# Pairs of score tiles that share a threshold and a reciprocal, in an attention and feed-forward kernel

## The chip, the core and the metric

The kernel runs on one core of a Trainium2 chip, as one program in one launch. The core has five engines that work through instruction lists of their own and meet at semaphores: TensorE (PE, matmuls), VectorE (DVE), ScalarE (ACT), GpSimd (POOL) and SyncE (SP, which issues DMAs). The metric is the device time of one execution in microseconds; the median of three runs of the kernel before is 1106.18 us (1106.06 to 1106.43).

## The reference

```python
def _attn_ref(q, k, v, tau):                      # q, k, v: 8 x 8 x 576 x 64, tau = 0.02
    scores = scale * np.matmul(q, k.transpose(0, 1, 3, 2))
    thresh = np.max(scores, axis=-1, keepdims=True) - tau
    scores = np.where(scores >= thresh, scores, -1000000000.0)
    scores = scores - np.max(scores, axis=-1, keepdims=True)
    attn = np.exp(scores)
    attn = attn / (np.sum(attn, axis=-1, keepdims=True) + 1e-09)
    return np.matmul(attn, v)
def _moe_ref(x, w_in, w_out):                     # x: 4608 x 512, w_in: 512 x 2048, w_out: 2048 x 512
    h = x @ w_in
    g = np.where(h >= 1, h, np.where(h <= -1, 0.0, (h + 1) ** 2 / 4))
    return g @ w_out
```

The attention output of each token, all heads beside each other, is the x of the second function. Only the scores within 0.02 of their row's maximum keep a weight.

## The kernel before

The eight batches go one after the other through attention, and the feed-forward part (FFN) follows them token group by token group, so that both are in flight together. Every fp32 factor is split into two fp16 parts, hi and lo, and a product is three fp16 matmuls (hi hi, hi lo, lo hi). Batch 0 alone computes its scores in fp32 (L987), since its split q and k aren't ready.

A score tile is 128 query rows by 576 keys; there are 36 a batch, 288 in all. Two tiles of the fp16 kind are computed together into the two PSUM score buffers (L998, 12 matmuls). `add_tile` then does for each tile by itself: the maximum with its scale on VectorE (`smax`, L1038), the threshold as one 128x1 addition on VectorE (`sthr`, L1042), the exponential on ScalarE (L1045), a mask with the row sum on VectorE, a reciprocal of 128x1 on VectorE, then normalisation and split. The table TILE picks the way of that tail:
- P (the default): the mask reads the scores in PSUM (`smask`, L1064), the reciprocal is L1074, GpSimd normalises (L1082) and takes the rest (L1090), ScalarE makes the hi part (L1087).
- R (batch 0 only): `smax` also writes a copy of the scores to SBUF, so PSUM is free early; the mask reads that copy (`mask_r`, L1050), and the denominator gets its epsilon in an operation of its own (L1078) ahead of its reciprocal (L1079).
- S: mask, hi and rest straight from PSUM, the mask (L1098) and the rest (`lo_s`, L1109) on VectorE, none of it on GpSimd.
- T: one tile that TensorE transposes (`turn_e`, L1129).

Every tile but T's is sent by a transposing DMA (SP, L1112). When a part's tiles are there, `add_av` multiplies with v (L1194; 30 matmuls of 320 columns for the wide parts), and the result is split into the x of the FFN (L1202, L1206). An FFN step is FFN1 (L1266, 12 matmuls per 128 hidden units), two ScalarE operations (L1272, L1275), the gate on VectorE (L1279), and the split of the gate's 512 columns: `ghi` on ScalarE (L1284) and `glo` on VectorE (L1289), each in two operations, one for each half of 256 columns, since the halves lie in buffers of different rings (ga, gb). FFN2 (L1311, matmuls of 512 columns) sums into one PSUM buffer, and the group's tokens are scaled and stored.

The weights arrive as float64 and are converted in 32 tiles of 512 KB; the table CONV picks the engine for each step of each tile, and two of these steps matter here: a rest on VectorE with two inputs from SBUF (`rest2`, L865) and one from PSUM (L884). FSCALE picks the engine of the FFN's eight scale chains.

The order of the work is written out by hand: ORDER lists the numbers of all operations. The class Plan walks it with a cost for each operation, gives out the buffers of each ring, computes a start for each, and issues the program in the order of these starts. An engine executes its own instructions strictly in that order.

Of the kernel before, what the change touches and what calls it, by code (L numbers as in the profile page):

```python
# [1372 lines left out]
```

## Time and profile before

| | |
|---|---|
| median of 3 runs | 1106.18 us |
| profiled execution | 1105.19 us, its span 1103.4 us |
| PE busy | 1066.5 us (97%) |
| DVE busy | 912.6 us (83%) |
| ACT busy | 865.5 us (78%) |
| POOL busy | 724.7 us (66%) |
| mean granted clock of PE | 0.983 of full |

The span runs from the first instruction to the last; the execution's time has 1.8 us more. A share of busy time is an average over the whole span, and the stages differ: a window of the trace shows an engine's busy time in one stretch, a wait shows what released an engine that stood idle. The rows below are of this one execution.

### The profile page before, as it was taken

What the parts mean: (1) busy time and instruction counts of PE and PEld (TensorE: products, weight loads), DVE (VectorE), ACT (ScalarE), POOL (GpSimd) and SP (SyncE); (2) the same over time, 40 slices, a digit from 0 to 9 for tenths busy, and PEclk for the clock granted to TensorE, in tenths of its full rate; (3) what the DMA queues carried; (4) which work ended last, traced back from release to release, by engine and by line L of the source; (5) the groups of instructions that cost most, each with busy time, mean ns of one, the idle gap of its engine ahead of it and who ended that gap; (6) DMA issues with size and microseconds to landing.
All of it is one profiled execution on the core that took longest, in us unless ns stands there. A gap on an engine that the chain in (4) does not pass through costs nothing.

```text
span 1103.4 us, 27341 instructions
## 1 busy us (share of the span) xinstructions
PE 1066.5 (97%) x9827; PEld 721.4 (65%) x9827; DVE 912.6 (83%) x2704; ACT 865.5 (78%) x1651; POOL 724.7 (66%) x829
## 2 busy tenths in 40 slices
PE   6778899999999999999999999999999999999998
PEld 4567557666776666765676676666676676666774
DVE  6999999899989898897998898798778788888231
ACT  6888879798878888888788887788678787687442
POOL 6899998678867787786676654785537577364000
PEclk9679999999999999999999999999999999999999
DMA  9996787858966876688665966597635757575000
GB/s 330 303 290 115 145 175 153 136 119 195 187 111 141 164 164 133 107 178 165 124 120 124 182 126 124 101 179 158 123 75 100 146 102 138 96 119 110 9 20 29
DMA packets 419321, 154.96 MB, mean 140 GB/s; under 512 B 398192, under 2 KB 398192, under 8 KB 419184
## 3 DMA queue, kind: packets, MB, share of 16 engines
q1 hardware_dynamic: 419184, 153.21, 67.7%
q8 instruction: 77, 1.26, 0.5%
q14 instruction: 60, 0.49, 0.1%
HBM read 45.09 MB, written 9.44 MB: 49 GB/s over the span
## 4 chain that ended last, share of the span: by engine, by line
PE 78%; DVE 8%; POOL 5%; issue 3%; DMA 3%; ACT 3%; SPq 0%; DVEq 0%; POOLq 0%; ACTq 0%
PE ph L1266 30%; PE acc L1311 28%; PE ph L1194 9%; PE s L998 9%; POOL e L1082 2%; POOL hl L1090 2%; DMA eT<-hl 2%; DVE e L1064 1%; DVE s L1038 1%; PE s L987 1%; POOL WO L862 1%; ACT hl L1087 1%; ACT e L1045 1%; DMA raw<-in_v_dram 0%; DMA vst<-vb 0%
## 5 line engine op out<-in xcount | busy, mean ns | idle before, releaser
L1266 PE MATMUL ph<-x,WI 128*128 128x256 f16 (+1 forms) x4032 | 401.5, 259 | 2.4 <-DVE x L1206 2.1
L1090 POOL TENSOR_TENSOR hl<-e,hl 128x576 f16<-128x576 f32 x272 | 351.5, 1302 | 71.7 <-ACT hl L1087 68.3
L1266 PEld LDWEIGHTS <-WI 128*128 128x128 f16 x4032 | 346.9, 99 | 61.8 <-issue 19.1
L1082 POOL TENSOR_SCALAR e<-e,sm 128x576 f32<-128x576 f32 x272 | 217.2, 806 | 166.9 <-DVE sm L1074 135.2
L1087 ACT ACTIVATE hl<-e 128x576 f16<-128x576 f32 x272 | 183.5, 681 | 65.6 <-POOL e L1082 54.9
L1038 DVE TENSOR_SCALAR_CACHE_REDUCE s<-s,pc 128x576 f32<-128x576 f32 x252 | 199.1, 821 | 36.9 <-PE s L998 35.7
L1045 ACT ACTIVATE e<-s,sm 128x576 f32<-128x576 f32 x273 | 196.6, 740 | 28.4 <-DVE s L1038 25.5
L1064 DVE SCALAR_TENSOR_TENSOR e<-s,sm,e 128x578 f32<-128x578 f32 x257 | 204.9, 815 | 14.7 <-ACT e L1045 10.8
L1311 PE MATMUL acc<-WO,ga 128*128 128x512 f16 x864 | 201.8, 379 | 1.8 <-DVE WO L884 1.5
L1279 DVE SCALAR_TENSOR_TENSOR ph<-ph,fcs,asq 128x512 f32<-128x512 f32 (+1 forms) x160 | 112.0, 700 | 61.0 <-ACT asq L1275 60.3
L1272 ACT ACTIVATE asq<-ph,fcs 128x512 f32<-128x512 f32 (+1 forms) x160 | 116.0, 736 | 49.6 <-PE ph L1266 47.1
L1311 PEld LDWEIGHTS <-ga 128*128 128x128 f16 x864 | 80.9, 98 | 93.7 <-issue 10.0
L1194 PE MATMUL ph<-eT,vst 128*64 128x320 f16 (+2 forms) x1928 | 123.1, 284 | 2.8 <-DMA eT<-hl 1.2
L1194 PEld LDWEIGHTS <-vst 128*64 128x64 f16 x1928 | 101.2, 113 | 27.1 <-issue 17.2
L998 PE MATMUL s<-kk,qq 64*128 64x288 f16 (+1 forms) x1680 | 117.0, 285 | 1.6 <-DVE e L1064 1.3
L998 PEld LDWEIGHTS <-qq 64*128 64x128 f16 (+1 forms) x1680 | 66.6, 96 | 52.0 <-issue 40.2
L1275 ACT ACTIVATE asq<-asq 128x512 f32<-128x512 f32 x144 | 90.6, 630 | 3.1
L1289 DVE SCALAR_TENSOR_TENSOR ga<-ph,fcs,ga 128x256 f16<-128x256 f32 (+1 forms) x160 | 70.8, 451 | 23.5 <-ACT WI L1284 8.8
L1284 ACT ACTIVATE ga<-ph,fcs 128x256 f16<-128x256 f32 (+1 forms) x160 | 70.0, 448 | 16.7 <-DVE ph L1279 12.9
L1311 PE MATMUL acc<-WO,gb 128*128 128x512 f16 x300 | 72.3, 379 | 0.0
L1311 PE MATMUL acc<-WO,WI 128*128 128x512 f16 x288 | 68.5, 379 | 0.0
L1311 PE MATMUL acc<-WO 128*128 128x512 f16 x276 | 65.5, 379 | 0.0
(187 smaller groups left out, 1172.1 us busy)
## 6 DMA issues: line engine op xcount, KB each, us to landing
raw<-in_v_dram SPq DMA_DIRECT2D x32, 288.0 KB, 4.0
WO<-in_moe_w_in_dram SPq DMA_DIRECT2D x16, 512.0 KB, 7.4
out_dram<-ob SPq DMA_DIRECT2D x32, 256.0 KB, 2.6
...
```

What stands on the lines that cost most here:

```text
L998: T.matmul(ap(s, s_ps)[r, f, :SH], ap(qb, qq)[h, ql, c : c + r.stop - r.start], ap(kb, kk)[h, kl, f * SH : (f + 1) * SH], start=ql == kl = ...
L1038: V.tensor_scalar(rows(how), sv(), c, None, ALU.mult, ALU.min, accum_out=t[:, 0:1])
L1045: A.activation(ev(), rows(how), AF.Exp, bias=ap(m, sm)[:, 0:1], scale=-1.0)
L1064: V.scalar_tensor_tensor(ev(SH + 1), sv(SH + 1), t[:, 2:3], ev(SH + 1), ALU.is_le, ALU.mult, accum_out=t[:, 3:4])
L1082: G.tensor_scalar(ev(), ev(), ap(m, sm)[:, 5:6], ESC, ALU.mult, ALU.mult)
L1087: A.activation(part2(0), ev(), AF.Copy)
L1090: G.tensor_tensor(part2(w), ev(), part2(0), ALU.subtract)
L1194: T.matmul(o[hd * D : (hd + 1) * D, :n], vt[:, k, hd * D : (hd + 1) * D], t[:, kb, x * n : (x + 1) * n], start=m == 0, stop=m == len(block ...
L1266: T.matmul(h[:, i], WTh["i"][:, u, wl * 512 + c * P : wl * 512 + (c + 1) * P], x[:, cc, xl, c0 : c0 + n].rearrange("p (t n) -> p t n", n=P ...
L1272: A.activation(tv()[:, :, c], hv()[:, :, c], AF.Relu, bias=fcs[:, b, q, 0 : 1], scale=fcs[:, b, q, 1 : 2])
L1279: V.scalar_tensor_tensor(hv()[:, :, c], hv()[:, :, c], fcs[:, b, q, 2 : 3], tv()[:, :, c], ALU.max, ALU.min)
L1311: T.matmul(ap(ab, accs), gv(h, gl)[:, x], WTh["o"][:, fc + i, wl * 512 : (wl + 1) * 512], start=fc + i == 0 and m == 0, stop=not left[0] a ...
```

## The change

`add_tile(j)` becomes `add_tiles(js)`: the two tiles whose scores are computed together go through the tail together and share one buffer of small columns (sm). The threshold of both is one operation of 128x2 (L1077 after), and so is the reciprocal (L1105, L1109, L1128) and, in the R and S ways, the denominator's epsilon (L1108, L1127). A new way Q is the old P; a pair with way P has its threshold on GpSimd. 288 thresholds on VectorE become 134 there (11 of 128x1, 123 of 128x2) and 16 on GpSimd. The masks and maxima stay one per tile; both masks now follow the threshold that both maxima feed.

The buffers of the gate's halves and the two weight arrays become one SBUF array, `halves`; the weights lie in it in reverse order (`at_`). A stride between any two half buffers can so be expressed, and `ghi` (L1343) and `glo` (L1347) are one operation of 128x2x256 per step, but in the groups that hold two batches' tokens, which keep four operations of 128x2x64. 320 operations of `glo` become 192.

All FFN scale chains run on GpSimd. The tables of ways are new: 25 tiles go the R way (15 before) and 9 the S way (15), none the T way, and 11 weight tiles have `rest2` (15). Plan gets a mark `port` for VectorE operations which it keeps apart from GpSimd's in its computed starts, and another model of TensorE's clock. ORDER is new from end to end.

```diff
 TILE = {
-    0: "T", 1: "R", 2: "R", 8: "R", 9: "R", 11: "R", 15: "R", 18: "R", 20: "R", 23: "R", 24: "R", 26: "S", 28: "R", 29: "R", 30: "R", 31:
+    1: "Q", 2: "R", 3: "R", 4: "R", 5: "R", 6: "S", 7: "S", 8: "R", 9: "R", 10: "R", 11: "R", 12: "Q", 14: "R", 15: "R", 16: "R", 18: "S",
...
-FSCALE = "GGGVGGGG"
+FSCALE = "GGGGGGGG"
...
 ORDER = [
-    2, 3, 5, 4, 862, 863, 864, 561, 0, 563, 571, 562, 564, 865, 7, 566, 866, 867, 573, 576, 944, 572, 567, 954, 868, 568, 6, 16, 945, 578, 852, 581,
+    6, 7, 877, 2, 3, 878, 0, 8, 559, 880, 879, 881, 887, 561, 9, 560, 574, 564, 575, 888, 900, 562, 890, 910, 576, 5, 4, 901, 889, 565, 891, 566, 882,
...
+            if o.port:
+                x = port["DVE" if o.eng == "POOL" else "POOL"]
+                if x[0] < t + o.cost and t < x[1]:
+                    t = x[1]
+                port[o.eng] = (t, t + o.cost)
...
+    NG4, NW = 4, NU + WOFF
+    halves = cp.tile([P, 2 * (NG4 + 2 * NW), FW], F16, name="halves")
+
+    def weights(n):
+        x = 2 * (NG4 + n * NW)
+        t = halves[:, x : x + 2 * NW, :].rearrange("p (u h) n -> p u (h n)", h=2)
+        return t, t.bitcast(F32)
...
-        def sthr():
-            t = ap(m, sm)
-            V.tensor_scalar(t[:, 2:3], t[:, 0:1], tcs[:, 2:3], None, ALU.add)
+        def cols(x):
+            return ap(m, sm)[:, 2 * x : 2 * x + n2]
...
+        def sthr(E):
+            E.tensor_scalar(cols(1), cols(0), tcs[:, 2:3], 1.0, ALU.add, ALU.mult)
...
         def sden():
-            t = ap(m, sm)
-            V.reciprocal(t[:, 5:6], t[:, 3:4])
+            V.reciprocal(cols(3), cols(2))
 
         def den_t():
-            t = ap(m, sm)
-            V.tensor_scalar(t[:, 3:4], t[:, 3:4], EPS, None, ALU.add)
-            V.reciprocal(t[:, 5:6], t[:, 3:4])
+            V.tensor_scalar(cols(2), cols(2), EPS, None, ALU.add)
+            V.reciprocal(cols(3), cols(2))
...
+            thr = plan.op("POOL", 0.245, partial(sthr, G), os, uses=[m]) if how == "P" else plan.op("DVE", 0.13, partial(sthr, V), os, uses=[m])
...
-            def glo(hv=hv, gv=gv, g=g, q=q):
-                for h in range(2):
-                    for b, c in segs(g):
-                        V.scalar_tensor_tensor(gv(h, 1)[:, :, c], hv()[:, 2 * h : 2 * h + 2, c], fcs[:, b, q, 3 : 4], gv(h, 0)[:, :, c], ALU.mult, ALU.subtract)
+            def both(l, qs=qs):
+                u, x = qs[0].slot, GB[qs[1].slot]
+                return halves[:, u : x + 1 : x - u, l * 256 : l * 256 + 256].rearrange("p h (k n) -> p h k n", n=P)
...
+            def glo(hv=hv, both=both, g=g, q=q):
+                for h, b, c in cols(g):
+                    V.scalar_tensor_tensor(both(1)[:, h, :, c], halved(hv)[:, h, :, c], fcs[:, b, q, 3 : 4], both(0)[:, h, :, c], ALU.mult, ALU.subtract)
```

What the new order moves is seen at three places. In the rows, an operation's output stands left of the arrow; s are score buffers in PSUM, sm the small columns, e the exponentials, ph and acc other PSUM buffers, qq and kk the split q and k, WI and WO (after: halves) the weights and gate halves.

The first place is VectorE at the second pair of fp16 score tiles of batch 1, from its maxima to its masks. Before:

```order
L1038 TENSOR_SCALAR s_62,sm_125<-s_62,pc_116 128x2x288
L1038 TENSOR_SCALAR s_61,sm_121<-s_61,pc_116 128x2x288
L1042 TENSOR_SCALAR sm_125<-sm_125,tcs 128x1
L1042 TENSOR_SCALAR sm_121<-sm_121,tcs 128x1
L1206 SCALAR_TENSOR_TENSOR x_105<-ph_65,x_105 128x256
L1206 SCALAR_TENSOR_TENSOR x_106<-ph_65,x_106 128x64
L1064 SCALAR_TENSOR_TENSOR e_90,sm_125<-s_62,sm_125,e_90 128x578
L1074 RECIPROCAL sm_122<-sm_122 128x1
L1056 MEMSET e_91 128x2
L1064 SCALAR_TENSOR_TENSOR e_91,sm_121<-s_61,sm_121,e_91 128x578
L1074 RECIPROCAL sm_125<-sm_125 128x1
L1074 RECIPROCAL sm_121<-sm_121 128x1
```

And after, the same pair:

```order
L1105 RECIPROCAL sm_116<-sm_116 128x2
L1247 SCALAR_TENSOR_TENSOR x_104<-ph_64,x_104 128x256
L1247 SCALAR_TENSOR_TENSOR x_105<-ph_64,x_105 128x64
L1074 TENSOR_SCALAR s_61,sm_113<-s_61,pc_107 128x2x288
L1074 TENSOR_SCALAR s_62,sm_113<-s_62,pc_107 128x2x288
L1247 SCALAR_TENSOR_TENSOR x_104<-ph_63,x_104 128x256
L1247 SCALAR_TENSOR_TENSOR x_105<-ph_63,x_105 128x64
L1077 TENSOR_SCALAR sm_113<-sm_113,tcs 128x2
L1090 MEMSET e_89 128x2
L1097 SCALAR_TENSOR_TENSOR e_89,sm_113<-s_61,sm_113,e_89 128x578
L1090 MEMSET e_90 128x2
L1097 SCALAR_TENSOR_TENSOR e_90,sm_113<-s_62,sm_113,e_90 128x578
```

Two thresholds of 128x1 have become one of 128x2, and it stands behind both maxima; the splits of x (L1206, L1247) stand between.

The second place is TensorE ahead of the pair of scores by which the prediction goes. Before, what stands between the first and the second pair of batch 1 is 24 matmuls of FFN2, and between the second and the third 12 more and 30 of attention times v:

```order
L998 MATMUL s_61<-kk_78,qq_82 128x288
L1311 LDWEIGHTS ga_110
L1311 MATMUL acc<-WO,ga_110 128x512
...
L1311 LDWEIGHTS WI
L1311 MATMUL acc<-WO,WI 128x512
L1194 LDWEIGHTS vst_88
L1194 MATMUL ph_64<-eT_98,vst_88 64x320
...
L998 LDWEIGHTS qq_82
L998 MATMUL s_62<-kk_78,qq_82 128x288
```

After, 48 matmuls of FFN1 (L1326) and three of a statistic (L599) stand between the second and the third pair:

```order
L1023 MATMUL s_62<-kk_75,qq_79 128x288
L1326 LDWEIGHTS halves
L1326 MATMUL ph_64<-x_101,halves 128x128
...
L599 LDWEIGHTS sel
L599 MATMUL ph_63<-pc_108,sel 128x2
L1023 LDWEIGHTS qq_79
L1023 MATMUL s_61<-kk_75,qq_79 128x288
```

Counted up to the second pair, 84 matmuls of FFN2 stand ahead in the order before; counted up to the third, 96. In the order after 36 stand ahead of the third pair. The FFN1 matmuls ahead are 384 in all three cases.

The third place is VectorE in the middle of the program, at one pair of tiles. Before:

```order
L1038 TENSOR_SCALAR s_61,sm_123<-s_61,pc_119 128x2x288
L1038 TENSOR_SCALAR s_62,sm_124<-s_62,pc_119 128x2x288
L1042 TENSOR_SCALAR sm_123<-sm_123,tcs 128x1
L1042 TENSOR_SCALAR sm_124<-sm_124,tcs 128x1
L1064 SCALAR_TENSOR_TENSOR e_90,sm_123<-s_61,sm_123,e_90 128x578
L1064 SCALAR_TENSOR_TENSOR e_92,sm_124<-s_62,sm_124,e_92 128x578
L1206 SCALAR_TENSOR_TENSOR x_106<-ph_64,x_106 128x256
L1206 SCALAR_TENSOR_TENSOR x_103<-ph_64,x_103 128x64
L1074 RECIPROCAL sm_123<-sm_123 128x1
L1279 SCALAR_TENSOR_TENSOR ph_65<-ph_65,fcs,asq_99 128x512
L1074 RECIPROCAL sm_124<-sm_124 128x1
```

And after:

```order
L1074 TENSOR_SCALAR s_62,sm_112<-s_62,pc_109 128x2x288
L1074 TENSOR_SCALAR s_61,sm_112<-s_61,pc_109 128x2x288
L1077 TENSOR_SCALAR sm_112<-sm_112,tcs 128x2
L1097 SCALAR_TENSOR_TENSOR e_88,sm_112<-s_62,sm_112,e_88 128x578
L1097 SCALAR_TENSOR_TENSOR e_89,sm_112<-s_61,sm_112,e_89 128x578
L1105 RECIPROCAL sm_112<-sm_112 128x2
L1347 SCALAR_TENSOR_TENSOR halves<-ph_63,fcs,halves 128x2x256
```

The pair's own VectorE instructions are six where they were eight, and the gate rest beside them (L1347, `halves`) is one operation of 128x2x256.

## Rows read from the trace of the kernel before

**Rows 1.** The page: span, busy us of each engine, granted clock by slices.
```profile
span 1103.4 us, 27341 instructions
...
PE 1066.5 (97%) x9827; PEld 721.4 (65%) x9827; DVE 912.6 (83%) x2704; ACT 865.5 (78%) x1651; POOL 724.7 (66%) x829
...
PEclk9679999999999999999999999999999999999999
```

**Rows 2.** PE's timeline, 146 to 172 us: start, us, engine, line.
```profile
150.23 0.91 PE L998 MATMUL s<-kk,qq 64*128 64x288 f16 x12
...
157.06 0.89 PE L998 MATMUL s<-kk,qq 64*128 64x288 f16 x11 [0.40 <-DVE e L1064]
...
161.52 2.23 PE L1194 MATMUL ph<-eT,vst 128*64 128x320 f16 x29 [0.62 <-DMA eT<-hl]
```

**Rows 3.** Windows: stretch, length, busy us of PE, PEld, DVE, ACT, POOL, clock.
```profile
0.00:10.00 10.00, 3.04 (x10) 1.86 (x11) 1.91 (x7) 2.72 (x4) 6.18 (x41) 1.00 0.75 242
...
0.00:163.70 163.70, 134.09 (x1235) 92.66 (x1237) 148.52 (x441) 130.74 (x248) 143.46 (x190) 0.90 0.87 228
...
400.00:500.00 100.00, 100.00 (x946) 68.42 (x943) 89.78 (x271) 84.28 (x162) 76.19 (x87) 1.00 0.75 148
```

**Rows 4.** PE's waits from 170 to 1050 us: total us, times, longest.
```profile
PE s L998 <- DVE e L1064: 0.9, 2, 0.6
PE ph L1194 <- DMA eT<-hl: 0.6, 2, 0.4
PE ph L1266 <- DVE x L1206: 0.4, 1, 0.4
PE ph L1266 <- DVE WI L1289: 0.3, 1, 0.3
```

**Rows 5.** The chain that ended last, one piece: start, us, what.
```profile
361.77 5.29 PE acc L1311 x24
```

**Rows 6.** DVE's groups by form: xcount | busy us, mean ns | idle before.
```profile
L1064 DVE SCALAR_TENSOR_TENSOR e<-s,sm,e 128x578 f32<-128x578 f32 x257 | 204.9, 815 | 14.7 <-ACT e L1045 10.8
L1038 DVE TENSOR_SCALAR_CACHE_REDUCE s<-s,pc 128x576 f32<-128x576 f32 x252 | 199.1, 821 | 36.9 <-PE s L998 35.7 <-POOL pc L534 0.6
...
L1289 DVE SCALAR_TENSOR_TENSOR ga<-ph,fcs,ga 128x256 f16<-128x256 f32 x128 | 61.1, 478 | 18.0 <-ACT WI L1284 7.5 <-ACT WO L1284 6.7 <-ACT gb L1284 3.2
L1042 DVE TENSOR_SCALAR sm<-sm,tcs 128x1 f32<-128x1 f32 x288 | 56.2, 208 | 1.3
L1074 DVE RECIPROCAL sm<-sm 128x1 f32<-128x1 f32 x257 | 38.1, 157 | 3.7
...
L1050 DVE SCALAR_TENSOR_TENSOR e<-raw,sm,e 128x576 f32<-128x576 f32 x15 | 15.7, 1048 | 0.3 <-ACT e L1045 0.2
...
L1098 DVE SCALAR_TENSOR_TENSOR s<-s,sm,e 128x576 f32<-128x576 f32 x15 | 12.2, 819 | 1.2 <-ACT e L1045 1.1
L1109 DVE SCALAR_TENSOR_TENSOR hl<-s,sm,hl 128x576 f16<-128x576 f32 x15 | 12.1, 814 | 3.0 <-ACT hl L1106 2.6
...
L865 DVE SCALAR_TENSOR_TENSOR WO<-WO,wsc_o 128x512 f16<-128x512 f32 x7 | 7.4, 1061 | 1.0 <-POOL WO L862 1.0
```

**Rows 7.** DVE's timeline from 26.9 to 29.8 us, two neighbours.
```profile
27.00 0.68 DVE L695 TENSOR_TENSOR vst<-ph,vst 128x512 f16<-128x512 f32 x1
27.60 0.81 DVE L1038 TENSOR_SCALAR_CACHE_REDUCE s<-s,tcs 128x576 f32<-128x576 f32 x1
```

**Rows 8.** Single lines of DVE: ns of one, least/median/most, then starts.
```profile
L1050 DVE SCALAR_TENSOR_TENSOR e<-raw,sm,e x15: 800/897/1804, 10.0 to 150.2; 128x576 f32<-128x576 f32 x15
...
L865 DVE SCALAR_TENSOR_TENSOR WO<-WO,wsc_o x7: 744/870/1758, 91.7 to 132.8; 128x512 f16<-128x512 f32 x7
...
L947 DVE TENSOR_SCALAR scs<-scs x8: 149/618/972, 23.0 to 903.1; 128x2 uint32<-128x2 uint32 x8
```

**Rows 9.** DVE and POOL in the timeline around one such operation.
```profile
270.40 0.74 DVE L947 TENSOR_SCALAR scs<-scs 128x2 uint32<-128x2 uint32 x1
...
269.89 1.23 POOL L657 TENSOR_SCALAR vb<-raw,scs 128x1152 f16<-128x1152 f32 x1
```

More of the change, by code (lines that the diff above doesn't have):

```diff
@@ L297, in join, with op @@
         return ops[0]
-    def op(self, eng, cost, fn, after=(), take=(), uses=(), work=None, behind=None, mode=0):
-        o = Op(eng, cost, fn, work, mode)
+    def op(self, eng, cost, fn, after=(), take=(), uses=(), work=None, behind=None, mode=0, port=False, share=1.0):
+        o = Op(eng, cost, fn, work, mode, port, share)
         o.n = len(self.ops)
@@ L667, in add_v @@
             o1 = plan.op("POOL", 1.197, hi, [so], take=[tb], uses=[rb])
[L668 removed]
+            o2 = plan.op("DVE", 0.735, lo, [o1], uses=[rb, tb], port=True)
             o3 = plan.op("SP", 1.65, send, [o2], take=[ob], uses=[tb], work=VSEND)
@@ L733, in w_scale @@
         so = plan.op("DVE", 0.62, scales, [ps], uses=[sb])
-        so2 = plan.op("DVE", *((0.085, more) if w == "o" else (0.27, more)), [so, c_op])
+        so2 = plan.op("DVE", *((0.085, more) if w == "o" else (0.27, more)), [so, c_op], port=True)
         db = plan.buf("dgw")
@@ L900, in add_w @@
                     if how == "D":
-                        done.append(plan.op("DVE", 0.68, rest2, [o]))
+                        done.append(plan.op("DVE", 0.68, rest2, [o], port=True))
                         read.append(done[-1])
@@ L1002, in score @@
         cost = (1.08, 1.1)[mixed] + 0.01 * (len(js) - 1) if full else (0.735, 0.76)[mixed] + 0.01 * (len(js) - 1)
-        o = plan.op("PE", cost, qk32 if full else qk, [x for y in own for x in y[3]], take=[y[0] for y in own], uses=[x for y in own for x in y[1:3]], mode=2 + mixed)
+        o = plan.op("PE", cost, qk32 if full else qk, [x for y in own for x in y[3]], take=[y[0] for y in own], uses=[x for y in own for x in y[1:3]], mode=2 + mixed,
+                    share=0.5 if full and len(js) == 1 else 1.0)
@@ new lines, in add_tiles, with col, sv, ev @@
+    def add_tiles(js):
+        score(js)
+        n2 = len(js)
+        m = plan.buf("sm")
+        nk = SP // P
+        T_ = [tiles[j] for j in js]
+        at = [t[0] for t in T_]
+        b = parts[at[0]][0]
+        w = S if b else SP
+        for i in at:
+            if i not in eTb:
+                eTb[i] = plan.buf("eT")
+                part_tr[i] = []
+        ss, cs = [scored[j][0] for j in js], [QK[parts[i][:2]] for i in at]
+        ee, xx = [plan.buf("e") for _ in js], [plan.buf("hl") for _ in js]
+        rr = [plan.buf("raw") for _ in js] if not b else None
+        dd = [plan.buf("dge") for _ in js] if not b else None
+        flat = TILE.get(js[0], "P") in "TR"
+        def col(x, k):
+            return ap(m, sm)[:, 2 * x + k : 2 * x + k + 1]
+        def cols(x):
+            return ap(m, sm)[:, 2 * x : 2 * x + n2]
+        def sv(k, w=SH):
+            return ap(ss[k], s_ps)[:, :, :w]
+        def ev(k, w=SH):
+            e = ap(ee[k], es)
+            if flat:
+                return e[:, :S].rearrange("p (f n) -> p f n", f=2)
+            return e[:, : 2 * (SH + 1)].rearrange("p (f n) -> p f n", f=2)[:, :, :w]
+        def rows(how, k):
+            return ap(rr[k], raw).rearrange("p (f n) -> p f n", f=2) if how == "R" else sv(k)
+        def smax(how, k):
+            v = T_[k][1]
+            cb = cs[k][0]
+            c = ap(cb, pc)[:, 24 + v : 25 + v] if cb else tcs[:, 3:4]
+            V.tensor_scalar(rows(how, k), sv(k), c, None, ALU.mult, ALU.min, accum_out=col(0, k))
+        def sthr(E):
+            E.tensor_scalar(cols(1), cols(0), tcs[:, 2:3], 1.0, ALU.add, ALU.mult)
+        def sexp(how, k):
+            A.activation(ev(k), rows(how, k), AF.Exp, bias=col(0, k), scale=-1.0)
+        def mask_r(k):
+            padded["e"].discard(ee[k].slot)
+            V.scalar_tensor_tensor(ev(k), rows("R", k), col(1, k), ev(k), ALU.is_le, ALU.mult, accum_out=col(2, k))
+        def pads(k):
+            e, s = ee[k], ss[k]
@@ L1114, in add_tile @@
-        take = [eTb[i]] if j == first[i] else []
-        d = plan.buf("dge") if not b else None
-        nk = SP // P
-        def view():
-            return ap(s, s_ps).rearrange("p f (k n) -> p (f k) n", n=P)[:, :nk]
-        def part(x0):
-            return ap(eTb[i], eT)[:, x0 : x0 + nk, col : col + P]
-        def diag():
-            G.tensor_scalar(ap(d, dge), ident, ap(m, sm)[:, 5:6], ESC, ALU.mult, ALU.mult)
-        def turn_e():
-            for k in range(nk):
-                T.matmul(view()[:, k], ap(e, es)[:, k * P : (k + 1) * P], ap(d, dge), start=True, stop=True)
@@ new lines, in view, with part, diag, turn_e @@
+        def view(k):
+            return ap(ss[k], s_ps).rearrange("p f (k n) -> p (f k) n", n=P)[:, :nk]
+        def part(k, x0):
+            return ap(eTb[at[k]], eT)[:, x0 : x0 + nk, T_[k][3] : T_[k][3] + P]
+        def diag(k):
+            G.tensor_scalar(ap(dd[k], dge), ident, col(3, k), ESC, ALU.mult, ALU.mult)
+        def turn_e(k):
+            for x in range(nk):
+                T.matmul(view(k)[:, x], ap(ee[k], es)[:, x * P : (x + 1) * P], ap(dd[k], dge), start=True, stop=True)
@@ new lines, in thi, with tlo @@
+        def thi(k):
+            A.activation(part(k, 0), view(k), AF.Copy)
+        def tlo(k):
+            V.tensor_tensor(part(k, nk), view(k), part(k, 0), ALU.subtract)
+        unit = ("tile", js[0])
+        ends = [[[], []] for _ in js]
+        lead = [i not in begun for i in at]
+        heads = [[] for _ in js]
+        for how in plan.ways(unit, TILE.get(js[0], "P"), "PQSTR" if not b else "PQS"):
+            os = []
+            for k in range(n2):
+                sb = [ss[k]] if how != "R" else [rr[k]]
+                cb = cs[k][0]
+                os.append(plan.op("DVE", 0.739, partial(smax, how, k), [scored[js[k]][1], cs[k][4]], take=([] if k else [m]) + ([rr[k]] if how == "R" else []),
+                                  uses=[ss[k], m] + ([cb] if cb else []), behind=os[0] if k else None))
+            exps = [plan.op("ACT", 0.632 if how != "R" else 0.68, partial(sexp, how, k), [os[k]], take=[ee[k]], uses=[ss[k] if how != "R" else rr[k], m]) for k in range(n2)]
+            thr = plan.op("POOL", 0.245, partial(sthr, G), os, uses=[m]) if how == "P" else plan.op("DVE", 0.13, partial(sthr, V), os, uses=[m])
+            if how == "S":
+                n = [plan.op("DVE", 0.748, partial(mask_s, k), [exps[k], thr], uses=[ss[k], m, ee[k]]) for k in range(n2)]
+                n = plan.op("DVE", 0.265, den_s, n, uses=[m])
+                done = []
+                for k in range(n2):
+                    o = plan.op("ACT", 0.64, partial(hi_s, k), [n], take=[xx[k]], uses=[ss[k], m])
+                    done.append(plan.op("DVE", 0.72, partial(lo_s, k), [o], uses=[ss[k], m, xx[k]]))
+            elif how == "T":
+                n = [plan.op("DVE", 0.748, partial(mask_t, k), [exps[k], thr], uses=[ss[k], m, ee[k]]) for k in range(n2)]
+                n = plan.op("DVE", 0.26, den_t, n, uses=[m])
+                for k in range(n2):
+                    i = at[k]
+                    o = plan.op("POOL", 0.355, partial(diag, k), [n, c_op], take=[dd[k]], uses=[m])
+                    o = plan.op("PE", 0.268 * nk, partial(turn_e, k), [o], uses=[ss[k], ee[k], dd[k]])
+                    o = plan.op("ACT", nk * P / 1200 + 0.05, partial(thi, k), [o], take=[eTb[i]] if js[k] == first[i] else [], uses=[ss[k], eTb[i]],
+                                behind=begun.get(i) or (heads[0][-1:] if k and at[0] == i else None))
+                    heads[k].append(o)
+                    ends[k][0].append(plan.op("DVE", nk * P / 960 + 0.065, partial(tlo, k), [o], uses=[ss[k], eTb[i]]))
@@ L1164, in add_tile @@
-                n = plan.op("POOL", 1.25, slo, [n], uses=[e, x])
-            if how != "T":
-                into.append(plan.op("SP", 1.36, send, [n], take=take, uses=[x, eTb[i]], work=SEND, behind=begun.get(i)))
-                parted.append(into[-1])
-        begun.setdefault(i, into)
-        part_tr[i].append(plan.join(parted))
+                    n = [plan.op("DVE", 0.74, partial(mask_r, k), [exps[k], thr], uses=[rr[k], m, ee[k]], port=True) for k in range(n2)]
+                    n = plan.op("DVE", 0.26, den_t, n, uses=[m])
+                else:
+                    n = [plan.op("DVE", 0.785, partial(smask, k), [exps[k], thr], uses=[ss[k], m, ee[k]]) for k in range(n2)]
+                    n = plan.op("DVE", 0.08 + 0.005 * (n2 - 1), sden, n, uses=[m])
@@ new lines, in add_tiles @@
+                done = []
+                for k in range(n2):
+                    o = plan.op("POOL", 0.72, partial(snorm, k), [n], uses=[ee[k], m])
+                    o = plan.op("ACT", 0.58, partial(shi, k), [o], take=[xx[k]], uses=[ee[k]])
+                    done.append(plan.op("POOL", 1.25, partial(slo, k), [o], uses=[ee[k], xx[k]]))
+            if how != "T":
+                for k in range(n2):
+                    i = at[k]
+                    o = plan.op("SP", 1.36, partial(send, k), [done[k]], take=[eTb[i]] if js[k] == first[i] else [], uses=[xx[k], eTb[i]], work=SEND,
+                                behind=begun.get(i) or (heads[0][-1:] if k and at[0] == i else None))
+                    heads[k].append(o)
+                    ends[k][0].append(o)
@@ L1171, in add_av @@
+        for k in range(n2):
+            begun.setdefault(at[k], heads[k])
+            part_tr[at[k]].append(plan.join(ends[k][0]))
     def add_av(i):
@@ L1221, in add_av @@
                 xdone[g, x].append(o)
+    left = {i: last[i] + 1 - first[i] for i in range(len(parts))}
     for j in range(NS):
-        add_tile(j)
-        i = tiles[j][0]
-        if j == last[i]:
+        js = together.get(j, [j])
+        if j != js[-1]:
+            continue
+        add_tiles(js)
+        for x in js:
+            left[tiles[x][0]] -= 1
+        while left and not left[min(left)]:
+            i = min(left)
+            left.pop(i)
             add_av(i)
```

194 lines of the change are left out of this document (74 added, 120 removed), and 397 rows, old and new, of tables (ORDER, TILE).

## The prediction, made before the changed kernel ran

> **What bounds the kernel now.** I read the page first, for the shares, and then looked for the place where the end is set. TensorE is busy 1066.5 of 1103.4 us [rows 1], so the whole program can lose at most the 37 us in which it is idle or late; the granted clock is below nine tenths only in slices 2 and 3. The list of PE's waits says where those 37 us lie: from 170 to 1050 us it waits four kinds of times, 0.9 + 0.6 + 0.4 + 0.3 = 2.2 us in all [rows 4], and in the stretch from 400 to 500 us it is busy 100.00 of 100 us with VectorE at 89.78 [rows 3]. From about 160 us on the order of PE is therefore worked off without a gap, and the program ends when the matmuls that are left at that point are done. Nothing that frees VectorE, ScalarE or GpSimd after that point can show in the time.
>
> The windows view then shows what holds PE before: up to 163.7 us PE is busy 134.1, VectorE 148.5, GpSimd 143.5 us [rows 3]. VectorE's 15.2 us without work are mostly its start (1.9 us of work in the first 10). PE's timeline gives the exact place: the second pair of score tiles of batch 1 starts its main part at 157.06 us, released by a mask on VectorE (L1064) after 0.40 us of waiting [rows 2]. That is the mark I use: at 157.06 us VectorE's order, PE's order and the clock on the wall meet. The time is then 157.06 plus 946.3 us for what stands behind it, of which 0.62 + 2.2 = 2.8 us is waiting [rows 2, 4].
>
> **The method.** For a matmul in the new order I count the VectorE instructions that must be over before it can start (through every semaphore), price each by the trace of before, and set that against the PE work which still stands behind the matmul. Prices are steps from one start to the next, a little below the means: a next instruction begins about 0.08 us before the one ahead ends (27.00 + 0.68 against 27.60) [rows 7]. In before the mark has 142.8 us of such VectorE work in front of it, and 157.06 - 142.8 = 14.3 us is start and idle. In after the matmul with nearly the same sum is the first of the third pair of batch 1: 142.3 us. So one compares these two.
>
> **VectorE's 142.3 us, part by part (after against before, up to the mark).**
> - Maxima 38 to 40: 2 x 0.79 = +1.6.
> - Masks: from PSUM (L1064) 20 to 7, from a raw copy in SBUF (L1050) 15 to 25, in the S way (L1098) 1 to 7, in the T way 1 to 0. With 0.76, 0.99, 0.82 and 0.68 a piece: -9.9 + 9.9 + 4.9 - 0.7 = +4.2. The S way leaves its rest on VectorE (L1109, 1 to 7 at 0.77) where the others leave it to GpSimd: +4.6, less 0.7 for the T tile's.
> - Rests of weight tiles (L865) 15 to 11 at 0.95, and one of L884: -4.4.
> - Thresholds: 37 of 128x1 become 11 of 128x1 and 14 of 128x2: 12 fewer x 0.13 = -1.6. Reciprocals and denominators together -0.4.
> - Gate halves: 14 of 256 columns at 0.44 become 6 of 512 at 0.70: -2.0. Two gates fewer: -1.3. All else (projections' rests, statistics): -0.4.
> - The sum is -0.4 us [means in rows 6]. The saving on VectorE is spent, before the mark, on tiles done the R and S ways.
>
> **PE's work behind the mark.** In the two orders the same 384 FFN1, 330 attention-value and 80 fp32 score matmuls stand ahead of it, but 84 FFN2 matmuls in before and 36 in after; 12 fp16 score matmuls more stand ahead in after. The 48 FFN2 matmuls come behind: 48 x 5.29/24 = +10.6 [rows 5]. The 12 scores are done: -0.91 [rows 2]. So at the same VectorE work PE has 9.7 us more to do, and no gap behind in which to hide it. The order has moved VectorE's cheaper operations to the long middle, where [rows 3] show that 10 us of each 100 are free anyway, and left the start with less finished FFN work.
>
> **Two costs that the trace of before bounds but doesn't show.**
> - 128x2 operations. Before the mark after has 25 tensor_scalars of 128x2 on VectorE (14 thresholds, 11 denominators) in fp32. Before has only 128x1 thresholds, which never wait (208 ns each), and eight 128x2 conversions (L947, uint32) that took 149 to 972 ns, mean 510 [rows 6, 8]. The longest lasted exactly to the end of a running GpSimd instruction: 270.40 + 0.74 against 269.89 + 1.23 [rows 9]. GpSimd is hardly ever idle before the mark. Lower end 0 (if fp32 with a pointer scalar behaves as 128x1 does), upper end 25 x (0.618 - 0.149) = 11.7 by the median; I take the mean, 25 x 0.36 = +9.0, since L947 is the nearest row in shape and place.
> - Collisions of two-input operations. The mask from the raw copy took 800 ns at best, 897 in the median and 1804 at worst, the weight rest 744, 870, 1758 [rows 8]; my prices are means and hold collisions at the rate of before. The new plan keeps such operations and GpSimd's apart. If the means fall to the medians, 25 x 0.15 + 11 x 0.19 = -5.8; if to the least, 25 x 0.25 + 11 x 0.3 = -9.6; if the plan fails, 0. I take -6.
>
> [...]
>
> **Sum.** The third pair starts at 157.06 - 0.4 + 9.0 - 6 = 159.7. Behind it: 946.3 + 9.7 - 2.8 (I give the waits of before back in full, since more PE work lies ahead of every consumer) = 953.2. Span 1112.9, against 1103.4. The profiled execution took 1105.19, 1.8 more than its span, and the median of the runs is 1106.18, 1.0 above it: 1112.9 + 1.8 + 1.0 = 1115.7, so **1116 us**, 0.9% slower.
>
> What costs nothing: the 16 thresholds on GpSimd (all but one behind the mark, where it idles a quarter: 76.19 of 100 [rows 3]); the 128 wide gate rests and the wide ScalarE halves in the middle; the reciprocals behind the mark (288 in all become 150, at 157 ns [rows 6]). They would count only if PE waited there.
>
> **Rivals.**
> - Faster, about 1101. Mechanism: the port plan works in the first 160 us. No 128x2 operation waits (-9.0), R masks and weight rests run at their least (a further -3.6), and some 2 us of VectorE's idle go: 1115.7 - 14.6 = 1101. For it: 128x1 thresholds never waited, 7 us of VectorE's idle before the mark lie after its first ten. Against: GpSimd is busy 143.5 of 163.7 us there, so there are few gaps to place anything in. It decides for faster once waits and collisions together fall 12 us below my sum. 25%.
> - No change, about 1106.5: 128x2 operations don't wait, collisions fall only to the medians, 1115.7 - 9.0. For it the same 208 ns rows; against it L947. 13%.
> - Slower still, about 1124: waits by the median (+2.7) and collisions at the old rate (+6). The 11 reciprocals of 128x2 wait too in the worst case, +4: 1128. 17%.
> - PE starts to wait in the middle, because the first tile's mask now waits for its pair's second maximum (0.74 to 0.82 us later) and, 16 times, for a threshold in GpSimd's queue. 124 pairs x 0.1 us would be +12 on any of these. VectorE's work lags PE's need by more with every 100 us (10 free), so I give it no share of its own but a part of the upper end.
>
> **Chances and range.** About 0.2% (2.2 us) is what a measurement here can tell from no change. Forecast (1109 to 1120) 45%, faster 25%, same 13%, slower still 17%; slower in all 62%. The range runs from the middle of the faster case to the waits by the median with collisions unchanged: 1100 to 1126. The forecast's own range is 1109 to 1120.
>
> **What would show it.** In the profile after, the third block of L1023 should start near 160 us, with 36 FFN2 matmuls ahead of it, and PE should have no waits worth naming behind it. The 128x2 form of L1077 should have a mean near 0.5 us (0.15 to 0.2 refutes the waits); L1084, the R mask, a median near 0.85. If that block starts below 148 us the step on VectorE's work is wrong; if it starts near 160 and the end is not later, the step on PE's gapless rest is.

## The result and the profile after

The changed kernel takes 1122.49 us (median of 4 runs, 1121.27 to 1123.31) where the kernel before takes 1106.31 beside it: a ratio of 1.0144 (95% interval 1.0126 to 1.0162), 16.2 us slower. The forecast was 1116 with a range of its own of 1109 to 1120, which the result misses by 2.5 us; the whole range, 1100 to 1126, holds it. The profiled execution took 1121.27 us with a span of 1119.5.

The first place to look is PE's timeline at the third score pair of batch 1 (start, us, engine, line; in brackets idle time and what released PE), the mark of the prediction:

```profile
158.16 0.28 PE L1023 MATMUL s<-kk,qq 64*128 64x288 f16 x1
158.96 0.90 PE L1023 MATMUL s<-kk,qq 64*128 64x288 f16 x11 [0.52 <-DVE e L1097]
161.06 2.84 PE L1326 MATMUL ph<-x,halves 128*128 128x128 f16 x48 [1.20 <-DVE x L1247]
...
165.39 0.91 PE L1023 MATMUL s<-kk,qq 64*128 64x288 f16 x11 [0.59 <-DVE e L1097]
```

The second pair's main part starts at 158.96, near the 157.06 it had before [rows 2], but less FFN work stands ahead of it. The third, which had as much VectorE work ahead as before's second, starts at 165.39 against a forecast of 159.7. Every wait here ended on VectorE. Behind the mark remain 1119.5 - 165.4 = 954.1 us, forecast 953.2. PE's waits from 170 to 1060 us (total us, times, longest) answer to [rows 4]:

```profile
PE ph L1326 <- DVE x L1247: 0.3, 1, 0.3
PE s L1023 <- DVE e L1097: 0.2, 1, 0.2
PE ph L1235 <- DMA vst<-vb: 0.2, 1, 0.2
```

There are 0.7 us of them, where before had 2.2. So PE has no gap behind the mark, and the 16.1 us of the span are made ahead of it, in two parts: the mark comes 8.3 us later, and 7.8 us more are left to do behind it (954.1 against 946.3). The windows of the two kernels up to their marks (stretch, length, busy us of PE, PEld, DVE, ACT, POOL, then clock, DMA share and GB/s), before's first:

```profile
0.00:157.10 157.10, 128.11 (x1182) 89.32 (x1184) 141.99 (x420) 126.75 (x240) 137.71 (x182) 0.89 0.87 229
```
```profile
0.00:165.40 165.40, 118.17 (x1133) 83.63 (x1133) 151.97 (x390) 116.84 (x216) 137.26 (x187) 0.88 0.89 219
```

Ahead of the mark VectorE is busy 10.0 us longer with 30 instructions fewer, and PE has done 9.9 us less. PE's total did not change, 1066.5 us before [rows 1] and 1066.3 after:

```profile
PE 1066.3 (95%) x9818; PEld 718.1 (64%) x9818; DVE 905.1 (81%) x2258; ACT 835.6 (75%) x1510; POOL 750.4 (67%) x880
```

So 1066.3 - 118.2 = 948.1 us of PE work stand behind the mark where before had 1066.5 - 128.1 = 938.4. VectorE's busy time ahead of the mark by line shows where its 10 us are. After, in this order: the thresholds on VectorE (L1077), the R masks with their accumulator reads (L1084), the weight rests (L890), the denominators of the R and S ways (L1108, L1127):

```profile
0.00:165.40 165.40, 9.82 (x25) 0.88 0.89 219
...
0.00:165.40 165.40, 28.26 (x50) 0.88 0.89 219
...
0.00:165.40 165.40, 14.03 (x11) 0.88 0.89 219
...
0.00:165.40 165.40, 3.78 (x16) 0.88 0.89 219
...
0.00:165.40 165.40, 1.62 (x5) 0.88 0.89 219
```

Before, the thresholds (L1042), R masks (L1050) and weight rests (L865):

```profile
0.00:157.10 157.10, 7.38 (x38) 0.89 0.87 229
...
0.00:157.10 157.10, 15.85 (x30) 0.89 0.87 229
...
0.00:157.10 157.10, 15.31 (x15) 0.89 0.87 229
```

A threshold took 0.39 us in the mean after and 0.19 before; an R mask with its accumulator read 28.26/25 = 1.13 against 1.06; a weight rest 1.28 against 1.02. The groups by form over the whole span answer to [rows 6] (xcount | busy us, mean ns | idle before):

```profile
L1077 DVE TENSOR_SCALAR sm<-sm,tcs 128x2 f32<-128x2 f32 x123 | 61.2, 497 | 2.5
...
L1084 DVE SCALAR_TENSOR_TENSOR e<-raw,sm,e 128x576 f32<-128x576 f32 x25 | 28.1, 1134 | 1.9 <-ACT e L1080 1.9
...
L1105 DVE RECIPROCAL sm<-sm 128x2 f32<-128x2 f32 x126 | 20.3, 161 | 3.1
...
L890 DVE SCALAR_TENSOR_TENSOR halves<-halves,wsc_o 128x512 f16<-128x512 f32 x8 | 10.1, 1260 | 0.0
...
L1077 DVE TENSOR_SCALAR sm<-sm,tcs 128x1 f32<-128x1 f32 x11 | 2.2, 202 | 0.0
...
L1074 DVE TENSOR_SCALAR_CACHE_REDUCE s<-s,pc 128x576 f32<-128x576 f32 x252 | 198.1, 820 | 67.9 <-PE s L1023 67.3 <-POOL pc L559 0.2
```

The same line took 497 ns at 128x2 and 202 at 128x1. The 128x2 reciprocal took 161 against 157 at 128x1 [rows 6], so it does not wait. The last row is of use further down. What the others wait for is seen at two places of the timeline, with GpSimd (POOL) and VectorE side by side:

```profile
112.44 1.19 POOL L875 TENSOR_SCALAR halves<-halves,wsc_o 128x512 f32<-128x512 f32 x1
113.00 0.66 DVE L1077 TENSOR_SCALAR sm<-sm,tcs 128x2 f32<-128x2 f32 x1
...
118.08 0.80 DVE L1084 SCALAR_TENSOR_TENSOR e<-raw,sm,e 128x576 f32<-128x576 f32 x1
118.16 1.85 POOL L1121 TENSOR_TENSOR hl<-e,hl 128x576 f16<-128x576 f32 x1
...
118.81 1.82 DVE L1084 SCALAR_TENSOR_TENSOR e<-raw,sm,e 128x576 f32<-128x576 f32 x1
```

The threshold ends at 113.66, 30 ns after GpSimd's operation at 113.63. Of two R masks in a row the first, begun just ahead of GpSimd's L1121, took its 0.80; GpSimd's operation, begun inside it, took 1.85 where its mean over the span is 1.30, and the second mask, begun inside that, took 1.82.

### The profile page after: what moved, and what is told of

Read it like the earlier page. It is cut to its first block, busy times and chain, and to the rows that moved or that the text cites. A ratio compares the mean times of both kernels' runs of the same rounds, so it can differ in the third digit from the quotient of the medians.

```text
span 1119.5 us, 26435 instructions
## 1 busy us (share of the span) xinstructions
PE 1066.3 (95%) x9818; PEld 718.1 (64%) x9818; DVE 905.1 (81%) x2258; ACT 835.6 (75%) x1510; POOL 750.4 (67%) x880
## 4 chain that ended last, share of the span: by engine, by line
PE 83%; DVE 8%; DMA 3%; POOL 3%; issue 2%; ACT 1%; SPq 0%; ACTq 0%; POOLq 0%; DVEq 0%
PE acc L1369 32%; PE ph L1326 31%; PE s L1023 9%; PE ph L1235 9%; DVE e L1084 1%; POOL hl L1121 1%; DMA eT<-hl 1%; DVE s L1074 1%; DMA halves<-in_moe_w_in_dram 1%; DVE halves L890 1%; DVE e L1097 1%; DMA kk<-in_k_dram 1%; DVE raw L1074 1%; DMA vst<-vb 1%; DVE sm L1077 0%
## 5 line engine op out<-in xcount | busy, mean ns | idle before, releaser
L1121 POOL TENSOR_TENSOR hl<-e,hl 128x576 f16<-128x576 f32 x279 | 359.8, 1297 | 128.1 <-ACT hl L1118 121.3
L1326 PE MATMUL ph<-x,halves 128*128 128x256 f16 (+1 forms) x4032 | 402.8, 259 | 2.3 <-DVE x L1247 1.5
L1369 PE MATMUL acc<-halves 128*128 128x512 f16 x1728 | 400.3, 379 | 0.4 <-DVE halves L890 0.4
L1326 PEld LDWEIGHTS <-halves 128*128 128x128 f16 x4032 | 349.9, 99 | 59.7 <-issue 10.4
L1369 PEld LDWEIGHTS <-halves 128*128 128x128 f16 x1728 | 159.5, 98 | 189.1 <-issue 22.4
L1074 DVE TENSOR_SCALAR_CACHE_REDUCE s<-s,pc 128x576 f32<-128x576 f32 x252 | 198.1, 820 | 67.9 <-PE s L1023 67.3
L1080 ACT ACTIVATE e<-s,sm 128x576 f32<-128x576 f32 x263 | 190.2, 739 | 73.0 <-DVE s L1074 54.7
L1347 DVE SCALAR_TENSOR_TENSOR halves<-ph,fcs,halves 128x512 f16<-128x512 f32 (+1 forms) x192 | 112.5, 609 | 24.0 <-ACT halves L1343 23.4
L1343 ACT ACTIVATE halves<-ph,fcs 128x512 f16<-128x512 f32 (+1 forms) x192 | 105.0, 578 | 29.1 <-DVE ph L1339 26.1
L1077 DVE TENSOR_SCALAR sm<-sm,tcs 128x2 f32<-128x2 f32 (+1 forms) x134 | 63.3, 473 | 2.5
L1012 PE MATMUL s<-kk,qq 64*128 64x288 f32 (+1 forms) x160 | 39.9, 539 | 25.5 <-DMA kk<-in_k_dram 8.2
L1243 ACT ACTIVATE x<-ph 128x256 f16<-128x256 f32 (+1 forms) x100 | 28.1, 319 | 26.9 <-PE ph L1235 26.7
```

The costliest lines, as they stand in the source:

```text
L1074: V.tensor_scalar(rows(how, k), sv(k), c, None, ALU.mult, ALU.min, accum_out=col(0, k))
L1080: A.activation(ev(k), rows(how, k), AF.Exp, bias=col(0, k), scale=-1.0)
L1121: G.tensor_tensor(part2(k, w), ev(k), part2(k, 0), ALU.subtract)
L1326: T.matmul(h[:, i], WTh["i"][:, at_(u), wl * 512 + c * P : wl * 512 + (c + 1) * P], x[:, cc, xl, c0 : c0 + n].rearrange("p (t n) -> p t n" ...
L1347: V.scalar_tensor_tensor(both(1)[:, h, :, c], halved(hv)[:, h, :, c], fcs[:, b, q, 3 : 4], both(0)[:, h, :, c], ALU.mult, ALU.subtract)
L1369: T.matmul(ap(ab, accs), gv(h, gl)[:, x], WTh["o"][:, at_(fc + i), wl * 512 : (wl + 1) * 512], start=fc + i == 0 and m == 0, stop=not left ...
```

## The experiments

Theory O is the prediction's, with the waits: the new order leaves VectorE as much to do before the mark and PE more behind it. Theory P blames the pairing itself, whatever the order. The first four runs cross forms with orders.

**New order, old forms.** In a_thr1 thresholds and denominators are 128x1 again:

```diff
-            E.tensor_scalar(cols(1), cols(0), tcs[:, 2:3], 1.0, ALU.add, ALU.mult)
+            for k in range(n2):
+                E.tensor_scalar(col(1, k), col(0, k), tcs[:, 2:3], 1.0, ALU.add, ALU.mult)
...
```

> The changed kernel, its order and tables kept, with each pair's threshold and denominator as two operations of 128x1 in place of one of 128x2 (reciprocals stay paired). Theory O (the new order leaves VectorE as much work before the third score pair of batch 1 and PE 9.7 us more behind it; pairing costs only its waits): ahead of that pair the 25 operations of 128x2 took 7.2 us more than 128x1 ones would, 25 more instructions cost 25 x 0.13 = 3.3, so about -4 us: 1118.5. L1077 falls back to about 205 ns. Theory P (sharing one operation between two tiles is itself the cause, the order is neutral): most of the 16 us comes back, 1106 to 1110.

It took 1116.88 us (1115.94 to 1117.84), 1.0082 of before (1.0055 to 1.0109), 5.6 us better than the change, where theory O had said about 4 and theory P most of the 16. The threshold's 257 instructions (ns least/median/most) no longer wait, and the third pair starts 3.8 us earlier:

```profile
L1078 DVE TENSOR_SCALAR sm<-sm,tcs x257: 193/207/223, 7.6 to 1028.2; 128x1 f32<-128x1 f32 x129
```
```profile
155.40 0.91 PE L1023 MATMUL s<-kk,qq 64*128 64x288 f16 x11 [0.52 <-DVE e L1098]
161.55 0.91 PE L1023 MATMUL s<-kk,qq 64*128 64x288 f16 x12
```

In a_narrow the reciprocals and gate halves are single as well (`ghi` and `glo` as before, `for k in range(n2)` around each reciprocal).

> As a_thr1, and also reciprocals of 128x1 and gate halves in two operations each: every per-tile form of before, under the new order and tables. Theory O: the 13 reciprocals and 6 gate halves ahead of the third pair cost about 1 us each kind, so 1120 to 1121, still 14 us above before. Theory P: 1106 to 1108.

It took 1118.61 us (1116.94 to 1119.35), 1.0095 (1.0072 to 1.0119). With every form as before, 12 of the 16 us remain, a little less than the 14 of theory O, where theory P had them gone. They belong to what is left of the change: the order, its tables, and one thing that no run here takes out of the new order, that a pair's two thresholds are issued together behind both maxima. The trace speaks against this last as a cause of the later start: ahead of the mark VectorE idles 165.4 - 151.97 = 13.4 us in the change and 157.1 - 141.99 = 15.1 in before.

**Old order, new forms.** b_pair keeps before's order and tables; an operation that a pair now shares moves to the second tile's place, and operations that depend on it are held until it is out:

```diff
-            V.tensor_scalar(t[:, 2:3], t[:, 0:1], tcs[:, 2:3], None, ALU.add)
+            V.tensor_scalar(cols(1), cols(0), tcs[:, 2:3], None, ALU.add)
...
-        for o in (self.ops[n] for n in ORDER):
+        while todo:
+            for o in todo:
...
+                if all(x in done for x in wants.get(o, [])) and all(len(free[p]) >= n for p, n in need.items()):
+                    break
```

> The kernel before with its own order and tables, and with one threshold, denominator and reciprocal per pair of tiles of the same way (128 pairs, all on VectorE). Theory O: 11 operations of 128x2 ahead of the second pair of batch 1 wait 0.29 us each (+3.1), 19 fewer instructions give back 2.1: about +1 us, 1107. Theory P: 1118 or more.

b_all has the wide gate halves too.

> As b_pair, and with the gate's halves in one array and one operation per step: all new forms under the old order and tables. Theory O: the 7 wide gate rests ahead of the mark save 0.17 us each, 1.2 in all: 1106, no change. Theory P: 1118 or more, as b_pair.

b_pair took 1150.60 us (1147.68 to 1153.08; 1.0385, 1.0356 to 1.0414) and b_all 1140.41 (1138.60 to 1140.71; 1.0291, 1.0267 to 1.0314). Theory O, with 1107 and 1106, failed in both, and theory P's bound of 1118 was met: under the old order the pairing by itself costs far more than its 128x2 waits ahead of the mark. b_pair's second pair waits until 160.78, 3.7 us after before's. Most is lost later, not at the start that theory O looked at; windows from 200 to 1100 us show PE in before, in the change, and in b_pair:

```profile
200.00:1100.00 900.00, 896.11 (x8234) 600.93 (x8228) 729.34 (x2164) 700.21 (x1339) 549.79 (x607) 1.00 0.65 124
```
```profile
200.00:1100.00 900.00, 899.18 (x8287) 603.86 (x8286) 719.03 (x1781) 685.83 (x1235) 581.92 (x655) 1.00 0.68 126
```
```profile
200.00:1100.00 900.00, 874.24 (x7953) 587.60 (x7950) 747.52 (x1915) 687.64 (x1316) 552.80 (x612) 1.00 0.65 125
```

PE idles 3.9, 0.8 and 25.8 us there. Its waits in b_pair from 170 us on, and then in the next run, b_rec:

```profile
PE s L1015 <- DVE e L1093: 21.8, 36, 2.3
```
```profile
PE s L1015 <- DVE e L1094: 12.2, 21, 1.9
```

Score matmuls wait for masks that come late. b_rec has the same pairs and order with thresholds and denominators of 128x1, and only the reciprocals shared:

> The kernel before with its own order and pairs as in b_pair, but thresholds and denominators as two operations of 128x1 each, issued where b_pair has one of 128x2; reciprocals are paired. b_pair lost 44 us, 26 of it as PE waiting for masks after 170 us. Theory W (the 128x2 operations wait for GpSimd, 128 times 0.36 us, and the old order has not that much VectorE lead): those waits are gone, 1106 to 1110, PE waits after 170 us under 5 us. Theory C (coupling: both masks stand behind both maxima, and the old order brings the second one late): 1135 or more, with the PE waits of b_pair.

It took 1137.28 us (1136.17 to 1138.96; 1.0286, 1.0271 to 1.0301). Of b_pair's 44 us, 13 are the 128x2 operations and 31 stay without them; theory W, with 1106 to 1110, is out. Theory C met its bound of 1135, though with 12.2 us of these waits where it expected the 21.8 of b_pair. PE's idle after 200 us grew by 13.5 us, the second pair came 2 us later, and the score matmuls were busy 9.4 us longer (112.2 + 14.2 against 104.0 + 13.0). Most of these 9.4 us are the same waits. In b_rec:

```profile
159.07 1.26 PE L1015 MATMUL s<-kk,qq 64*128 64x288 f16 x12
...
173.21 0.29 PE L1015 MATMUL s<-kk,qq 64*128 64x288 f16 x1
174.09 0.89 PE L1015 MATMUL s<-kk,qq 64*128 64x288 f16 x11 [0.58 <-DVE e L1094]
```

Twelve matmuls in a row without a wait took 0.91 us [rows 2], a step of less than 0.08 each. A first matmul that stands alone is recorded with 0.29 us, so up to 0.2 us of the wait for the second score buffer count as busy in each such block. In b_rec 40 of the 112 blocks of twelve take more than 1.0 us, in before 10, and what counts so as busy adds up to 8.6 us more. So an order made for single tiles pays when its pairs are coupled, and that is shown; some 6 of the 31 us are not located. Which part of the coupling does it is open: in b_rec both masks stand behind both maxima, both normalisations behind the shared reciprocal, and other operations shift with them.

**One form alone on the old order.** With the wide gate halves b_all is 10 us faster than b_pair, for a reason that no run isolates. b_wide has only the wide gate halves (the `halves` array and the `ghi` and `glo` of the change).

> The kernel before with the gate's halves in one array and one operation per step on ScalarE and VectorE, and nothing else. Theory O (only VectorE's work ahead of the second pair of batch 1 counts): 7 gate rests there save 0.17 us each, so -1.2 us, 1105; what it saves in the middle does not show. Rival: the wide form delays FFN2's first half, which now waits for the whole split, and PE waits in the middle: 1108 or more.

It took 1109.71 us (12 runs, 1105.40 to 1112.11), 1.0028 (1.0016 to 1.0039). Its second pair starts at 157.77, not earlier, and of PE's waits after 170 us 4.5 us are for masks:

```profile
PE s L1009 <- DVE e L1075: 4.5, 6, 1.7
```

The rival's bound was met, but not by its mechanism: the waits are for masks and not for FFN2's halves. Theory O, with 1105, failed; why the masks come later here is not shown.

**GpSimd silenced.** A collision is here a VectorE and a GpSimd operation that overlap and make each other longer: in the trace of the change the 19 R masks that began while a GpSimd operation ran took 1236 ns in the mean, the other 6 took 812. They are measured by a cut of GpSimd's rest in batches 0 and 1 to 2 columns a tile, in the change (a_quiet) and in before (b_quiet); both kernels so leave out the lo parts there, whose buffers they zero once at the start:

```diff
-            G.tensor_tensor(part2(k, w), ev(k), part2(k, 0), ALU.subtract)
+            c = slice(0, 1) if b <= 1 else slice(0, SH)
+            G.tensor_tensor(part2(k, w)[:, :, c], ev(k)[:, :, c], part2(k, 0)[:, :, c], ALU.subtract)
```

> The changed kernel with GpSimd's rest (L1121) of batches 0 and 1 cut to 2 columns a tile, so that their lo parts are left out; some 28 instructions of 1.30 us go from GpSimd before the third pair, a quarter of its busy time. [...]

> The kernel before with the edit of a_quiet: GpSimd's rest (L1090) of batches 0 and 1 cut to 2 columns a tile, their lo parts left out. Theory G (what a_quiet gained, 11 us, was collisions of VectorE with GpSimd, of which the changed kernel has more): before the mark this kernel has 15 masks from the raw copy at +0.25 and 15 weight rests at +0.29 over their least, 8 us, and no 128x2 thresholds, so it gains less than half of 11: -2 to -5 us. Rival (GpSimd's own chain is what held the changed kernel): as much as there, -9 or more.

One execution each: 1111.10 us, 11.4 below the change, and 1101.48, 4.8 below before. Up to a_quiet's third pair the R masks fell to 24.17 us (28.26 in the change) and the weight rests to 9.61 (14.03):

```profile
0.00:155.50 155.50, 24.17 (x50) 0.90 0.95 233
...
0.00:155.50 155.50, 9.61 (x11) 0.90 0.95 233
```
```profile
155.49 0.91 PE L1022 MATMUL s<-kk,qq 64*128 64x288 f16 x11 [0.59 <-DVE e L1096]
```

The 14 thresholds of 128x2 fell from 7.7 us to 5.7 and the 11 denominators of 128x2 from 4.0 to 2.6. VectorE's busy time up to the pair went from 151.97 us to 138.57, its idle time up by 3.5, and the third pair came 9.9 us earlier and the end 10.2. In b_quiet VectorE's busy time up to the second pair went from 141.99 us to 133.33, and that pair, at 151.48, came 5.6 us earlier. Since VectorE's own operations became shorter while its idle time grew, theory G holds for both and not its rival. The change gets back more, 13.4 us of VectorE's time against 8.7, although less was taken from GpSimd: its rests ahead of the mark went from 40.9 us to 9.2 there, and from 44.9 to 7.5 in b_quiet.

**VectorE relieved.** b_act and a_act put the first 42 tiles' thresholds on ScalarE:

```diff
-            V.tensor_scalar(t[:, 2:3], t[:, 0:1], tcs[:, 2:3], None, ALU.add)
+            if j < 42:
+                A.activation(t[:, 2:3], t[:, 0:1], AF.Identity, bias=tcs[:, 2:3], scale=1.0)
...
```

> The kernel before with the thresholds of its first 42 tiles on ScalarE (an addition as an activation of 128x1 with a bias) in place of VectorE; everything else and the order kept. Theory O (the time is set by VectorE's work ahead of the second pair of batch 1): 37 thresholds of 0.13 us leave VectorE there, 4.8 us; ScalarE idles a fifth of that stretch and takes about 0.2 us for each. If half of the saving survives as waits for ScalarE: -2.4 us; in full -4.8, 1101.5. Rival: the mask now waits longer for ScalarE (exponential and threshold one after the other), VectorE stands still instead, 1106 or more.

> The changed kernel with the thresholds of its first 42 tiles (11 of 128x1, 15 pairs of 128x2) on ScalarE. Theory O: 25 thresholds that took 9.9 us on VectorE ahead of the third pair leave it, so the third pair starts up to 9.9 us earlier and the end with it: 1113 to 1116. Rival (the pair's coupling, not VectorE's time, holds the start): within 3 us of 1122.

b_act was slower, 1115.25 us (1114.35 to 1116.78; 1.0087, 1.0072 to 1.0102). Up to its second pair at 160.8 VectorE was busy 138.24 us, 3.8 less than before, but idle 22.6 instead of 15.1; part of that is

```profile
DVE e L1053 <- ACT sm L1043: 3.0, 3, 1.7
```

So the rival was right there. a_act took 1118.97 (1118.67 to 1119.46), 3.5 us better than the change; its third pair started at 161.42, 4.0 earlier, and both expectations failed, 1113 to 1116 as well as within 3 us of 1122. Thresholds of 9.8 us left VectorE, but its busy time up to the pair fell by 7.4 only (144.57 us), and its idle time grew by 3.4. The denominators of 128x2 took 6.0 us instead of 4.0 and the R masks 1178 ns in the mean instead of 1134, while the weight rests became 3.3 us shorter.

b_eps leaves out the addition of 1e-9 in the R and T ways of before:

> The kernel before without the addition of 1e-9 to the row sums of its 16 R and T tiles (L1078), sums that are at least 1; nothing else changed. Theory O: 16 operations of 128x1 leave VectorE ahead of the second pair of batch 1, at 0.12 us from start to start 1.9 us in all: pair and end 1.5 to 2 us earlier, 1104.2 to 1105. Rival: VectorE's start is held by others (ScalarE, GpSimd, the arriving weights), no change.

It gained nothing: 1109.67 us (12 runs, 1105.49 to 1110.90), 1.0018 (1.0001 to 1.0035). The second pair's main part began at 158.68, 1.6 us later than before's, the R masks took 1120 ns in the mean instead of 1048 and the weight rests 15.69 us instead of 15.31. VectorE's busy time up to the pair was 142.45 us against 141.99, although 2.3 us of additions had gone: R masks 1.1 us, conversions of weight scales (128x2) 0.6, rests of k 0.5 and weight rests 0.4 longer took it back, all of them operations with two SBUF inputs or 128x2 ones. That the removal moved them against GpSimd's operations is the likely reading; no run shows it by itself. No version here that computes the whole result beat the kernel before.

## Why the prediction was right, step by step

- **PE is dense behind the mark.** Right. What followed the third pair was nearly the same whatever came ahead: 954.1 us in the change, 1115.0 - 161.55 = 953.5 in a_thr1, 1117.5 - 163.49 = 954.0 in a_narrow, 1109.3 - 155.49 = 953.8 in a_quiet; a_act had 1117.6 - 161.42 = 956.2. The forecast was 953.2.
- **The order's debt.** Right. Behind the mark PE has 948.1 - 938.4 = 9.7 us more work, which is the 9.7 that the prediction counted; with less idle time there the stretch is 954.1 - 946.3 = 7.8 us longer, forecast 9.7 - 2.8 = 6.9. a_narrow shows that the debt stays with the old forms.
- **The 128x2 operations wait.** Right, and a little smaller: 25 thresholds took 9.82 us where 25 x 0.202 = 5.05 would be due at 128x1, and 21 denominators 5.40 where 21 x 0.143 = 3.0 were due: +7.2, forecast +9.0. a_thr1 gave back 5.6 us of time. The +9.0 was an estimate from the eight uint32 rows of L947 (mean 510 ns), and the fp32 rows came near them: 497 ns at 128x2, with 202 at 128x1 on the same line. GpSimd is what they wait for: of the 123 thresholds of 128x2 in the trace of the change, the 26 that began with no GpSimd operation running took 224 ns in the mean and the other 97 took 571; each of the 71 that took over 0.1 us more than the least (215 ns) ended within 0.05 us of the end of a GpSimd operation; and in a_quiet 14 of them took 5.7 us instead of 7.7. Of the 288 thresholds of 128x1 before, 218 began with one running and took 208 ns like the others; why the wide form alone waits is not shown. The reciprocal of 128x2, for which the rival "slower still" kept +4 us, did not wait (161 ns). One reading was inexact: the 0.74 us at 270.40 is not the longest L947 of before; that is one of 0.97 us at 22.98, and it too ends, at 23.95, within 0.02 us of a GpSimd operation (L859, 22.77 + 1.16).
- **The collisions.** Wrong, the one failed term. "The new plan keeps such operations and GpSimd's apart" was taken at -6 us. They grew instead, R masks by 28.26 - 25 x 1.057 = +1.8 and weight rests by 14.03 - 11 x 1.02 = +2.8, which is 10.6 us from the term; the R mask's median was 926 ns where 0.85 us was to be the sign. The plan keeps starts apart that it computes itself, and the R mask at 118.81 and L1121 at 118.16 met all the same. Less waiting of 128x2 operations (-1.8), less idle time of VectorE (13.4 against 15.1, -1.7) and other prices (-1.4) leave 5.7 us of the 10.6: the third pair's 165.39 against 159.7.
- **The size.** The measured 1122.49 is 6.8 us above the sum of 1115.7: 5.7 at the mark, 0.9 behind it and 0.2 in the runs. It lies above the forecast's own range of 1109 to 1120, near the slower case of 1124 that had 17%, but not by the split of that case: the waits were smaller than the forecast's and not larger, and the collisions were worse than the old rate at which it put them. That 4.9 us of smaller errors went the other way was luck; without them the result would lie near 1127, outside the whole range.
- **The middle.** PE's waits there fell to 0.7 us, so the forecast held, but its reason is not enough. The prediction named the coupling of a pair's tiles and gave it no share of its own, because VectorE has 10 us free in each 100. The old order has the same room, and b_rec loses 31 us with the coupling. What differs is how far VectorE is ahead: it stood idle for the next scores 67.3 us in the change (the L1074 row), 35.7 in before [rows 6] and 22.9 in b_rec. That the new order bought this lead with its start is a reading and not shown by a run.
